# Unused bytes between the buffers of a weight ring, in a fused attention and two-MLP kernel

## The chip, the cores and the metric

One core of a Trainium2 chip runs the whole kernel in one launch. The metric is the device time of that core in microseconds (us). The engines are TensorE (PE; its weight loads are shown as a row of their own, PEld), VectorE (DVE), ScalarE (ACT), GpSimd (POOL) and SyncE (SP), which issues every DMA here.

## The reference, cut to what matters

```python
def _attn_ref(q, k, v):                    # 2 x 12 heads, 448 tokens, head size 64
    scores = where(causal, q @ k.T / 8, -1e9)
    return softmax(scores) @ v

x = attn_out.reshape(896, 768)

def _moe_ref(x, w_in, w_out):              # 768 -> 2048 -> 768
    h = x @ w_in
    return (h * sigmoid(h)) @ w_out

def _moe2_ref(x, w_in, w_out, g_ln):       # 768 -> 1024 -> 768
    h = x @ w_in
    solu = h * softmax(h)
    return (layernorm(solu) * g_ln) @ w_out
```

All in float32. The weights arrive from the host as 64-bit words, and are float64 in value.

## The kernel before, in words

The kernel runs in five stages: the attention, then four matrix products called GEMM1 to GEMM4 here. To keep the precision of float32, each operand of a GEMM is split into a high and a low part in the matmul type fp32r, and each product is three matmuls: high by high, high by low, low by high.

GEMM1 (`gemm1`, lines 304 to 312) multiplies the weights w1 with the attention's result. The weights are the **stationary** operand (loaded into the array, 128 by 128), and the activations `xh` and `xl` are the **moving** operand (448 columns, one batch half). GEMM2 (`mm2`, lines 486 to 492) does the same with w2 and the activations `gh` and `gl`. Each of the two has 96 weight blocks of 128x128, and each block meets two batch halves with three matmuls, so there are 2 x 96 x 2 x 3 = 1,152 matmuls of 448 columns in all, 576 in each GEMM. In GEMM3 (line 606) and GEMM4 (line 661) the sides are changed: the activations are stationary and the weights move, from tiles of their own that stay in place.

The weights of GEMM1 and GEMM2 pass through a **ring**. Each is cut into 32 chunks of 384 columns (three blocks). A chunk is loaded by DMA (`load_w`), put together from its 64-bit words on ACT (line 216) and DVE (lines 221, 227, 237), and split by `split_w` (line 239): ACT writes the high part `wh` (line 247), POOL writes the low part `wl` (line 248). Both come from the pool `wring`, which has 4 buffers for each name, 1,536 bytes per partition each, so that successive chunks take successive buffers and a buffer comes free when the last matmul on the chunk before it in that buffer has read it. All four buffers of a name lie a multiple of 256 bytes apart, since 1,536 is 6 x 256.

The order of the work is written out by hand (`feed`, `feed_to` and the loops from line 437 on). Chunks go round the ring in order; each chunk is used for one batch half (9 matmuls), then for the other (9 matmuls). The first four chunks of GEMM1 and the last four of GEMM2 are visited once for each half at different times.

The kernel already places unused bytes at six spots (`pad`, line 60): they shift the tiles behind them. As the program is built, the activations `xh`, `xl`, `gh` and `gl` start at 224 modulo 256 bytes in a partition and all ring buffers at 160, so the distance from the moving operand to the stationary one is 192 modulo 256 in every matmul of GEMM1 and GEMM2 (steps from block to block and from half to half are multiples of 256). In GEMM3 the moving weights start at 32 and the stationary activations at 224, which is again a distance of 192, with 512 columns. In GEMM4 both start at 0, a distance of 0, with 256, 384 or 512 columns. The transposes of line 641 have a distance of 128.

Of the kernel before, what the change touches and what calls it, by code (L numbers as in the profile page):

```python
# [8 lines left out]
F32 = mybir.dt.float32  # L9
F32R = mybir.dt.float32r  # L10
# [17 lines left out]
CH = 384  # L28
# [15 lines left out]
def fused(ctx, tc, qT, kT, vv, vt, w1, w2, w3, w4, gl, out):  # L44
# [3 lines left out]
    def pool(name, bufs=1, **kw):  # L48
        return tc.alloc_tile_pool(name=name, bufs=bufs, **kw)
# [3 lines left out]
    raw = pool("raw", RAWS)  # L53
    xs = pool("xs", XS)
    gap = pool("gap")
    wring = pool("wring", 4)

    ident = const.tile([128, 128], F32, name="ident")

    def pad(where, count):  # L60
        where.tile([128, count // 4], F32, name="pad", tag="pad", bufs=1)

    pad(act, 64)
    pad(gap, 192)
    xh = act.tile([128, KD, T], F32R, name="xh", tag="ah")
# [3 lines left out]
    with tc.manual_schedule():  # L69
# [169 lines left out]
        def split_w(n, c, dst=None, lo_engine=None):  # L239
            x = wx.pop((n, c))  # L240
            if dst is None:
                h = wring.tile([128, CH], F32R, name="wh", tag="wh")
                l = wring.tile([128, CH], F32R, name="wl", tag="wl")
                wsp[n, c] = (h, l)
            else:
                h, l = dst
            nc.scalar.activation(h, x, AF.Copy)  # L247
            (lo_engine or nc.gpsimd).tensor_tensor(l, x, h.bitcast(F32), ALU.subtract)  # L248
# [22 lines left out]
        def finish(m):  # L271
            n, c = order[m]
            if n < 3:
                split_w(n, c)
            elif n == 4:
                split4(c)
            ready.add(order[m])
# [78 lines left out]
        for i in range(NP2 + TL + 2):  # L356
            live = i < NP2
            n, r, p, x = i - 1, i - TL, i - TL - 1, i - TL - 2
# [180 lines left out]
        for m in range(N3):  # L539
            if m == 10:  # L540
                for a in tail:
                    block2(a, 1)
                evict2(yps[KD - 1, 1], KD - 1, 1)
            sl = slice(CH * m, CH * m + CH)
            split_w(3, m, (w3h[:, sl], w3l[:, sl]), nc.vector if m % 3 else nc.gpsimd)
# [194 lines left out]
```

## Time and profile before

| | |
|---|---|
| median of 3 runs | 442.62 us (442.28 to 442.82) |
| the profiled execution's own time | 442.5 us |
| its span, first to last instruction | 440.7 us |
| what lies around the span | 1.8 us |
| PE, PEld, DVE, ACT, POOL busy | 98%, 87%, 73%, 51%, 39% of the span |

A matmul's duration in the profile (363 ns for 448 columns) runs from its start to the drain of its last column, and the next one starts long before that. The spacing of the starts, read from the timeline, is what a matmul costs here. The stages follow each other: attention until about 90 us, with GEMM1 from there to 200 us, GEMM2 to 315 us, GEMM3 to 374 us and GEMM4 to the end.

### The profile page before, as it was taken

How to read it: one execution, taken by the hardware profiler on the slowest of the kernel's cores; microseconds unless marked ns; L12 is line 12 of the kernel's file. 1: busy time of each engine (PE TensorE's matmuls, PEld its weight loads, DVE VectorE, ACT ScalarE, POOL GpSimd, SP SyncE). 2: the span in 40 equal slices, each digit the busy share in tenths (PEclk: the TensorE clock that was granted, in tenths of full speed). 3: DMA queues.
4: the chain of work that ended last, by engine and by line, in shares of the span. 5: the costliest groups of instructions: out<-in, count | busy, mean ns of one | idle time of the engine just before them, and what ended most of it. 6: DMA issues, size and time to landing. Idle time of an engine off the chain costs nothing.

```text
span 440.7 us, 6969 instructions
## 1 busy us (share of the span) xinstructions
PE 432.4 (98%) x2379; PEld 382.2 (87%) x2379; DVE 321.9 (73%) x705; ACT 223.5 (51%) x519; POOL 170.3 (39%) x197
## 2 busy tenths in 40 slices
PE   8899999999999999999999999999999999999997
PEld 5576777789999999999999999999888888999996
DVE  4988987679999999898785979756978787511110
ACT  4999998344443534344344444433647765712121
POOL 3757655137767777674432424332501000000000
PEclk9999999999999999999999999999999999999999
DMA  5787311205433434333745647564023210010101
GB/s 163 206 251 208 107 37 30 80 0 147 141 110 106 141 83 135 106 111 107 230 136 174 196 150 231 167 188 132 12 72 108 83 61 1 36 37 36 56 36 55
DMA packets 26387, 49.22 MB, mean 112 GB/s; under 512 B 6128, under 2 KB 13936, under 8 KB 26352
## 3 DMA queue, kind: packets, MB, share of 16 engines
q1 hardware_dynamic: 26352, 48.77, 36.8%
q8 instruction: 19, 0.31, 0.3%
q14 instruction: 16, 0.13, 0.1%
HBM read 46.01 MB, written 2.75 MB: 111 GB/s over the span
## 4 chain that ended last, share of the span: by engine, by line
PE 91%; ACT 4%; DVE 4%; issue 0%; DVEq 0%; ACTq 0%
PE h L312 8%; PE h L311 8%; PE h L310 8%; PE h L492 7%; PE h L491 7%; PE h L490 7%; PE ps L663 4%; PE ps L661 4%; PE ps L662 4%; PE h L608 4%; PE h L607 4%; PE h L606 4%; PE pv L193 4%; PE tr L165 3%; ACT e L142 3%; PE sa L125 2%
## 5 line engine op out<-in xcount | busy, mean ns | idle before, releaser
L248 POOL TENSOR_TENSOR wl<-wx,wh 128x384 fp32r<-128x384 f32 x64 | 77.6, 1212 | 95.4 <-ACT wh L247 91.8
L216 ACT ACTIVATE wr<-wr 128x384 f32<-128x384 f32 x96 | 52.5, 554 | 34.5 <-DMA wr<-w_in 34.2
L247 ACT ACTIVATE wh<-wx 128x384 fp32r<-128x384 f32 x64 | 33.5, 523 | 69.8 <-DVE wx L227 40.4
L227 DVE SCALAR_TENSOR_TENSOR wx<-wr,wx 128x384 uint32<-128x384 uint32 x96 | 66.6, 694 | 0.0
L312 PE MATMUL h<-xh,wl 128*128 128x448 f32 x174 | 63.2, 363 | 0.0
L311 PE MATMUL h<-xl,wh 128*128 128x448 f32 x174 | 63.1, 362 | 0.0
L310 PE MATMUL h<-xh,wh 128*128 128x448 f32 x174 | 62.6, 360 | 0.0
L237 DVE TENSOR_SCALAR wr<-wr 128x384 uint32<-128x384 uint32 x96 | 59.6, 621 | 4.1 <-DMA wr<-w_in 4.0
L221 DVE SCALAR_TENSOR_TENSOR wx<-wr 128x384 uint32<-128x384 uint32 x96 | 58.3, 608 | 1.3 <-POOL gl L320 1.3
L492 PE MATMUL h<-gh,wl 128*128 128x448 f32 x160 | 58.1, 363 | 0.0
L491 PE MATMUL h<-gl,wh 128*128 128x448 f32 x160 | 58.0, 362 | 0.0
L490 PE MATMUL h<-gh,wh 128*128 128x448 f32 x160 | 57.6, 360 | 0.0
L320 POOL TENSOR_TENSOR gl<-sg,gh 128x448 fp32r<-128x448 f32 x32 | 40.9, 1279 | 20.7 <-DVE gh L319 10.5
L142 ACT ACTIVATE e<-e,st 128x384 f32<-128x384 f32 (+3 forms) x84 | 43.7, 525 | 8.2 <-DVE st L136 8.2
L152 POOL TENSOR_TENSOR e<-e,st 128x384 f32<-128x384 f32 (+3 forms) x63 | 37.5, 629 | 26.7 <-PE tr L165 16.6
L661 PE MATMUL ps<-w4h,lh 128*128 128x384 f32 (+2 forms) x112 | 38.0, 339 | 0.0
L663 PE MATMUL ps<-w4h,ll 128*128 128x384 f32 (+2 forms) x112 | 37.5, 335 | 0.0
L662 PE MATMUL ps<-w4l,lh 128*128 128x384 f32 (+2 forms) x112 | 37.5, 335 | 0.0
L650 DVE TENSOR_TENSOR ll<-tp,lh 128x512 fp32r<-128x512 f32 x14 | 9.0, 686 | 37.3 <-ACT lh L649 37.3
L311 PEld LDWEIGHTS h<-xl,wh 128*128 128x128 f32 x174 | 32.7, 188 | 2.4
L310 PEld LDWEIGHTS h<-xh,wh 128*128 128x128 f32 x174 | 32.5, 187 | 2.3
L312 PEld LDWEIGHTS h<-xh,wl 128*128 128x128 f32 x174 | 32.7, 188 | 1.8
(100 smaller groups left out, 844.4 us busy)
## 6 DMA issues: line engine op xcount, KB each, us to landing
wr<-w_in SPq DMA_DIRECT2D x96, 384.0 KB, 3.6
k<-kT_in SPq DMA_DIRECT2D x12, 224.0 KB, 3.0
q<-qT_in SPq DMA_DIRECT2D x12, 192.0 KB, 3.1
v<-vv_in SPq DMA_DIRECT2D x12, 192.0 KB, 2.9
out<-o SPq DMA_DIRECT2D x12, 192.0 KB, 1.8
qt<-qT_in SPq DMA_DIRECT2D x24, 16.0 KB, 2.6
v<-vt_in SPq DMA_DIRECT2D x12, 32.0 KB, 2.5
out<-o SPq DMA_DIRECT2D x1, 256.0 KB, 2.0
```

Source lines behind the costliest of these rows:

```text
L142: nc.scalar.activation(ep(p, u), ep(p, u), AF.Exp, bias=st[p][:, 0, n:n + 1], scale=-1.0, accum_out=st[p][:, 1, n:n + 1])
L221: nc.vector.scalar_tensor_tensor(x.bitcast(U32), r[:, :, 1], 0x80000000, r[:, :, 0], ALU.bitwise_and, ALU.bitwise_or)
L227: nc.vector.scalar_tensor_tensor(xu, r[:, :, 1], 3, xu, ALU.logical_shift_left, ALU.bitwise_or)
L237: nc.vector.tensor_scalar(low, low, 29, None, ALU.logical_shift_right)
L248: (lo_engine or nc.gpsimd).tensor_tensor(l, x, h.bitcast(F32), ALU.subtract)
L310: nc.tensor.matmul(ps[:, :S], wh, rh, start=k == 0, stop=False)
L311: nc.tensor.matmul(ps[:, :S], wh, rl, start=False, stop=False)
L312: nc.tensor.matmul(ps[:, :S], wl, rh, start=False, stop=k == KD - 1)
L490: nc.tensor.matmul(ps[:, :S], wh, rh, start=f == 0, stop=False)
L491: nc.tensor.matmul(ps[:, :S], wh, rl, start=False, stop=False)
L492: nc.tensor.matmul(ps[:, :S], wl, rh, start=False, stop=f == KF - 1)
L661: nc.tensor.matmul(ps[:, :w], lh[:, k], w4h[:, k, ns], start=k == 0, stop=False)
```

## The change

The pool `wring` no longer rotates four buffers under one name. Eight tiles are allocated once, four for `wh` and four for `wl`, and `split_w` takes them in turn. Behind each tile lie unused bytes: 32, 96, 96 and 32 for the four of a part, in sum 256.

```diff
-    wring = pool("wring", 4)
+    wring = pool("wring")
...
+    ring = {"wh": [], "wl": []}
+    for part in ring:
+        for space in (32, 96, 96, 32):
+            ring[part].append(wring.tile([128, CH], F32R, name=f"{part}{len(ring[part])}", tag=f"{part}{len(ring[part])}"))
+            wring.tile([128, space // 4], F32, name="pad", tag=f"{part}p{len(ring[part])}")
+    turn = [0]
     pad(act, 64)
     pad(gap, 192)
...
             if dst is None:
-                h = wring.tile([128, CH], F32R, name="wh", tag="wh")
-                l = wring.tile([128, CH], F32R, name="wl", tag="wl")
+                h, l = ring["wh"][turn[0] % 4], ring["wl"][turn[0] % 4]
+                turn[0] += 1
                 wsp[n, c] = (h, l)
```

As built, the four tiles of a part start at 160, 192, 32 and 128 modulo 256, so the distance from the moving operand (224) is 192, 224, 64 and 160 for successive chunks; it is the same for the high and the low part of a chunk. Each distance belongs to 16 of the 64 chunks, which is 288 of the 1,152 matmuls. The ring as a whole grows by 512 bytes, so what lies behind it keeps its place modulo 256. On each of the five engines the instructions and their order are those of before, and so are the number, the semaphores' engines and the values of the waits.

## Rows read from the trace of the kernel before

**Rows 1.** The page: busy time and share of the span of each engine.
```profile
PE 432.4 (98%) x2379; PEld 382.2 (87%) x2379; DVE 321.9 (73%) x705; ACT 223.5 (51%) x519; POOL 170.3 (39%) x197
```

**Rows 2.** The whole answer on who PE waited for (total us, times, longest).
```profile
PE tr L165 <- ACT aT L183: 1.8, 3, 1.2
PE pv L326 <- DVE xl L322: 1.4, 1, 1.4
PE sb L125 <- DVE st L136: 0.7, 2, 0.5
PE pv L193 <- ACT aT L183: 0.7, 1, 0.7
PE sa L125 <- DVE st L136: 0.3, 1, 0.3
```

**Rows 3.** Windows: stretch, busy us (instructions) by engine, clock, DMA share, GB/s.
```profile
core 0: us, PE busy (x) PEld busy (x) DVE busy (x) ACT busy (x) POOL busy (x), PEclk, DMA share, GB/s
100.00:200.00 100.00, 100.00 (x502) 93.73 (x501) 95.28 (x146) 40.90 (x85) 70.13 (x58) 1.00 0.39 118
200.00:310.00 110.00, 110.00 (x552) 103.11 (x551) 83.21 (x156) 47.00 (x94) 39.49 (x32) 1.00 0.57 173
```

**Rows 4.** Timeline of PE in GEMM1: start, us, what; first and last of a stretch.
```profile
99.16 0.36 PE L310 MATMUL h<-xh,wh 128*128 128x448 f32 x1
...
196.36 0.36 PE L310 MATMUL h<-xh,wh 128*128 128x448 f32 x1
```

**Rows 5.** Line 310 between 99.16 and 196.35 us: matmuls, ns min/median/max, first and last start.
```profile
L310 PE MATMUL h<-xh,wh x162: 360/360/360, 99.2 to 195.8; 128*128 128x448 f32 x162
```

**Rows 6.** Timeline of PE in GEMM3: first and last of a stretch.
```profile
339.92 0.39 PE L606 MATMUL h<-w3h,yh 128*128 128x512 f32 x1
...
360.52 0.39 PE L606 MATMUL h<-w3h,yh 128*128 128x512 f32 x1
```

**Rows 7.** Line 606 between 339.92 and 360.51 us.
```profile
L606 PE MATMUL h<-w3h,yh x30: 388/388/388, 339.9 to 359.8; 128*128 128x512 f32 x30
```

**Rows 8.** Timeline of PE in GEMM4, its 512-column slice, and what follows.
```profile
429.04 0.39 PE L661 MATMUL ps<-w4h,lh 128*128 128x512 f32 x1
429.27 0.40 PE L662 MATMUL ps<-w4l,lh 128*128 128x512 f32 x1
429.50 0.40 PE L663 MATMUL ps<-w4h,ll 128*128 128x512 f32 x1
429.74 0.39 PE L661 MATMUL ps<-w4h,lh 128*128 128x512 f32 x1
429.96 0.39 PE L662 MATMUL ps<-w4l,lh 128*128 128x512 f32 x1
430.20 0.40 PE L663 MATMUL ps<-w4h,ll 128*128 128x512 f32 x1
430.43 0.39 PE L661 MATMUL ps<-w4h,lh 128*128 128x512 f32 x1
430.66 0.40 PE L662 MATMUL ps<-w4l,lh 128*128 128x512 f32 x1
430.89 0.39 PE L663 MATMUL ps<-w4h,ll 128*128 128x512 f32 x1
431.12 0.39 PE L661 MATMUL ps<-w4h,lh 128*128 128x512 f32 x1
...
434.52 0.28 PE L661 MATMUL ps<-w4h,lh 128*128 128x256 f32 x1
```

**Rows 9.** The chain that ended last: start, us, what; transposes of 128 columns.
```profile
364.80 0.87 PE tp L641 x8
```

**Rows 10.** The ring's writers: who waited for whom (total us, times, longest).
```profile
POOL wl L248 <- ACT wh L247: 91.8, 42, 6.2
ACT wh L247 <- DVE wx L227: 40.4, 20, 3.7
ACT wh L247 <- PE h L311: 21.8, 14, 2.6
```

## The prediction, made before the changed kernel ran

> **What bounds the kernel now.** I read the busy shares first: PE is busy 98% of the span, the next engine, DVE, 73% [rows 1]. A high busy share of PE can hide gaps, so the second view is who PE waited for. That answer has five rows, all of them on attention lines, 4.9 us in sum, and none on a ring buffer [rows 2]. In GEMM1 and GEMM2 PE is busy in every microsecond of the two windows, at a granted clock of 1.00, which is the 2.4 GHz level [rows 3]. The writers of the ring are the ones that wait: POOL for ACT, ACT for DVE, and ACT for matmuls to set a buffer free [rows 10]. So the two GEMMs that the change touches last exactly as long as the spacing of their matmul starts, and nothing but that spacing can move the time, unless the feeding engines become late.
>
> The third view is the spacing itself. In GEMM1, line 310 starts 162 times between 99.16 and 196.36 us [rows 4, 5]; with lines 311 and 312 that is 486 matmuls in 97.20 us, or **200.0 ns for 448 columns**. At one column a cycle, 448 columns at 2.4 GHz last 186.7 ns, so each matmul pays 13.3 ns on top. GEMM2 does the same: 552 matmuls touch its window of 110.00 us, two of them at its edges [rows 3], which is 200 ns again. In GEMM3, also at distance 192, 90 matmuls of 512 columns take 20.60 us [rows 6, 7], 228.9 ns each; 512 columns last 213.3 ns, so the surplus is 15.6 ns. In GEMM4's last slice, at distance 0, the 24 matmuls start with nine in 2.08 us (231.1 ns each, surplus 17.8) and settle to 15 in 3.40 us (226.7 ns each, surplus 13.3) [rows 8].
>
> **The change part by part.** *Instructions, waits and queues:* none is added, removed or moved on any engine, DMA issues included, and the waits are the same in number and value. Eight fixed tiles in turn come free at the same matmuls as four rotating buffers did. I cost this at nothing. *The writers:* ACT and POOL write the same 384 columns to tiles that start 32, 128 and 224 bytes further modulo 256. Should a write get slower, the cover is their own waiting, 91.8 us of POOL and 40.4 plus 21.8 us of ACT [rows 10]; if the cover were gone, PE would wait for `wl` or `wh` in rows that are absent today.
>
> *The addresses:* the moving stream and the load of the next weights read the same partitions at the same time. A quarter of the matmuls, 288, keeps distance 192 and its 200.0 ns. The other 864 get distances 224, 64 and 160, which the trace has nowhere for fp32r. The bounds come from the nearest rows.
>
> - Below: the surplus of 13.3 ns need not be a floor. The plain fp32 transposes, at distance 128, take 0.87 us for eight [rows 9], 108.8 ns each; at two cycles a column 128 columns last 106.7 ns, which leaves a surplus of 2.1. So a distance could give back up to 13.3 - 2.1 = 11.2 ns.
> - Above: a distance at which the surplus doubles would cost 13.3 ns.
> - Between: GEMM3 settles 228.9 - 226.7 = 2.2 ns above GEMM4 at the same width, and the unsettled start of GEMM4's slice runs 231.1 - 226.7 = 4.4 ns above it.
>
> That 13.3 ns appears exactly, at distance 192 with 448 columns and at distance 0 with 512, makes it look like what remains when the two streams have settled without meeting; GEMM3 then shows a distance and width that settle less well. I take GEMM3's 2.2 ns for each of the three new distances, because it is the only settled spacing above that level: 864 x 2.2 = **1.9 us**.
>
> *The borders:* PE now changes distance at each change of chunk. 64 chunks, eight of them visited twice, make 72 visits and 71 borders. If streams have to settle anew, the row nearest is the start of GEMM4's slice: 2.08 us where nine settled matmuls take 2.04, so 0.04 us at most, and nothing at least. Half of that at 71 borders is **1.4 us**.
>
> The sum is 1.9 + 1.4 = 3.3 us on the profiled execution's 442.5 us: **445.8 us**. The median of the runs, 442.62 us, is 0.1 above that execution, which changes nothing here. A measurement of this kernel can tell about 0.2%, 0.9 us, from no change.
>
> What hides is little: PE is the bound, so added spacing goes to the end in full, and the feeders gain slack. Late next, if PE got faster, is DVE, 95.28 us busy in 100 us of GEMM1 [rows 3].
>
> **The rivals.**
>
> *No effect.* The surplus is the same 13.3 ns at distances 0 and 192 and at widths of 448 and 512, which speaks for a fixed cost without regard to address; GEMM3's extra 2.2 ns would then come from something else in that stage. The time would be 442.5 us. Against it stands that plain fp32 pays only 2.1 ns, so the surplus depends on how fast the moving operand is read, as a meeting of two streams would. The unsettled start of GEMM4's slice, in the same stage with the same code, speaks against it too. The case in which the spaces do not lead to different distances gives the same time; the addresses of the built program leave it no chance. The Trainium skill, "TensorE: Matmul & The Clock Gate", section "Part 2: What happens when you issue a matmul", says that TensorE reads the moving operand and the weights through two independent ports, so that loading the next weights takes no read bandwidth from the running matmul. By that rule this rival would be certain, with 442.5 us; the trace disagrees in part, since a matmul with a load beside it is 13.3 ns over its columns in fp32r.
>
> *Faster.* The 13.3 ns are the meeting of the two streams, and 192 and 0 are both bad distances. One good distance among the three gives back 288 x 11.2 = 3.2 us (439.3 us); all three 9.7 us (432.8 us), near where DVE's 95% would stop GEMM1. It decides for faster from a mean of 0.8 ns gained over the 1,152 matmuls. For it: fp32's 2.1 ns. Against it: two different distances give the same surplus, and every other mean spacing of fp32r matmuls read above lies over it.
>
> *One very bad distance.* A distance at which the loads always meet the stream doubles the surplus: 288 x 13.3 = 3.8 us, with 576 x 2.2 = 1.3 for the others and 1.4 for the borders 6.5 us, so 449.0 us. Nothing in the trace shows such a spacing settled; the single intervals in GEMM4's start reach 0.24 us against 0.227.
>
> **How the numbers follow.** Slower by over 0.2%: 0.60, of which 0.47 for the forecast with its bounds (0.9 us up to 864 x 4.4 + 71 x 0.04 = 6.6 us, so 443.4 to 449.1) and 0.13 for very bad distances (449.0, and 452.2 were it two: 576 x 13.3 + 288 x 2.2 + 1.4 = 9.7 us). No effect within 0.2%: 0.26. Faster: 0.14. The range leaves out the faster rival and the far end of very bad distances, under 0.2 together: 441.9 to 450.0 us. The likeliest case's own range is 443.4 to 449.1.
>
> **What would show it right or wrong.** Right: in GEMM1's timeline the 18 starts of a chunk, 3.60 us today, fall into four classes that repeat with every fourth chunk; one stays near 3.60, others are longer by about 0.04 us (18 x 2.2 ns), with the first matmuls of a chunk above the rest. GEMM3, GEMM4 and the attention keep their lengths. DVE, ACT and POOL keep the length of one instruction, and PE still waits for no ring buffer. Wrong on the size: a class 0.24 us longer (18 x 13.3 ns). Wrong on the mechanism: all chunks at 3.60 us (no effect), a class below 3.60 us (faster), or a wait of PE for `wh` or `wl`, which would make the writers the cause.

## The result, and the profile after

The changed kernel takes **446.58 us** (446.48 to 446.71, four runs) against 442.63 us before: a ratio of 1.0087, 95% interval 1.0073 to 1.0101. It is slower by 3.95 us; the span of its profiled execution grew from 440.7 to 444.7 us.

Busy time on the page of the changed kernel, to be set against [rows 1]:

```profile
PE 436.4 (98%) x2379; PEld 382.5 (86%) x2379; DVE 321.5 (72%) x705; ACT 223.6 (50%) x519; POOL 170.0 (38%) x197
```

The instructions are as many as before. PE's busy time grew by 4.0 us, as much as the span, and no other compute engine's by more than 0.1. So neither a wait nor a slower writer is the cause, and the next two views say the same. The first is who PE waited for, which has the same five lines and the same sums as [rows 2]; the first of the five:

```profile
PE tr L171 <- ACT aT L189: 1.8, 3, 1.2
```

The second is the writer of the ring's high part (ns min/median/max); before, its median on ACT was 526 ns too, and the median of POOL's low part is 1,137 ns in both traces:

```profile
L253 ACT ACTIVATE wh<-wx x64: 504/526/528, 37.2 to 304.9; 128x384 fp32r<-128x384 f32 x64
```

The time is in the spacing. The windows that answer to [rows 3] still have PE busy throughout, with 494 and 543 matmuls in them instead of 502 and 552:

```profile
100.00:200.00 100.00, 100.00 (x494) 92.30 (x493) 93.14 (x143) 41.27 (x86) 69.06 (x58) 1.00 0.40 118
200.00:310.00 110.00, 110.00 (x543) 101.50 (x542) 84.19 (x156) 45.10 (x89) 39.66 (x32) 1.00 0.56 166
```

PE's timeline in GEMM1 shows where. Each of these rows is the first matmul of a chunk (18 matmuls); the distances in turn are 192, 224, 64, 160, twice over, and the last row begins the next round:

```profile
128.81 0.36 PE L316 MATMUL h<-xh,wh 128*128 128x448 f32 x1
...
132.41 0.37 PE L316 MATMUL h<-xh,wh 128*128 128x448 f32 x1
...
136.09 0.36 PE L316 MATMUL h<-xh,wh 128*128 128x448 f32 x1
...
139.73 0.37 PE L316 MATMUL h<-xh,wh 128*128 128x448 f32 x1
...
143.43 0.36 PE L316 MATMUL h<-xh,wh 128*128 128x448 f32 x1
...
147.03 0.37 PE L316 MATMUL h<-xh,wh 128*128 128x448 f32 x1
...
150.74 0.37 PE L316 MATMUL h<-xh,wh 128*128 128x448 f32 x1
...
154.38 0.37 PE L316 MATMUL h<-xh,wh 128*128 128x448 f32 x1
...
158.08 0.36 PE L316 MATMUL h<-xh,wh 128*128 128x448 f32 x1
```

| distance | us a chunk, first round | second round | over 3.60 |
|---|---|---|---|
| 192 | 3.60 | 3.60 | 0 |
| 224 | 3.68 | 3.71 | 0.08 and 0.11 |
| 64 | 3.64 | 3.64 | 0.04 |
| 160 | 3.70 | 3.70 | 0.10 |

This pair of rounds repeats through both GEMMs, except at the two ends, where a chunk is visited for one batch half at a time. Sixteen rounds, half with 0.22 us and half with 0.25, come to 3.76 us by these readings. Counted from the first start of GEMM1 to the last of GEMM2, the trace itself grew by 3.6 us (from 241.1 us, 73.88 to 314.96, to 244.7 us, 74.10 to 318.83), of the span's 4.0.

### The profile page after: what moved, and what is told of

Its sections match the earlier page's. It is cut to its first block, busy times and chain, and to the rows that moved or that the text cites. A ratio compares the mean times of both kernels' runs of the same rounds, so it can differ in the third digit from the quotient of the medians.

```text
span 444.7 us, 6969 instructions
## 1 busy us (share of the span) xinstructions
PE 436.4 (98%) x2379; PEld 382.5 (86%) x2379; DVE 321.5 (72%) x705; ACT 223.6 (50%) x519; POOL 170.0 (38%) x197
## 4 chain that ended last, share of the span: by engine, by line
PE 91%; ACT 4%; DVE 4%; issue 0%; DVEq 0%; ACTq 0%
PE h L316 8%; PE h L317 8%; PE h L318 8%; PE h L496 7%; PE h L497 7%; PE h L498 7%; PE ps L669 4%; PE ps L667 4%; PE ps L668 4%; PE h L613 4%; PE h L614 4%; PE h L612 4%; PE pv L199 4%; PE tr L171 3%; ACT e L148 3%; PE sa L131 2%
## 5 line engine op out<-in xcount | busy, mean ns | idle before, releaser
L316 PE MATMUL h<-xh,wh 128*128 128x448 f32 x174 | 63.6, 365 | 0.0
L496 PE MATMUL h<-gh,wh 128*128 128x448 f32 x160 | 58.5, 366 | 0.0
```

The costliest lines, as they stand in the source:

```text
L316: nc.tensor.matmul(ps[:, :S], wh, rh, start=k == 0, stop=False)
L496: nc.tensor.matmul(ps[:, :S], wh, rh, start=f == 0, stop=False)
```

## The experiments

The question was what a chunk's spacing follows from. Theory A: from its own distance. Theory B: from the change of distance between chunks. Theory C: fixed tiles cost something in place of rotating buffers. More came up as results arrived, among them D, a distance has one or several settled spacings and the way PE enters picks one, and F, the address of the tile itself and not its distance from the moving operand.

### One distance for all chunks: 192, 224, 64, 160

The tiles lie without spaces, shifted together; `s` is 0, 32, 128 and 224.

```diff
-        for space in (32, 96, 96, 32):
...
+    wring.tile([128, s // 4], F32, name="pad", tag="front")      # none where s is 0
+    for part in ring:
+        for n in range(4):
+            ring[part].append(wring.tile([128, CH], F32R, name=f"{part}{n}", tag=f"{part}{n}"))
+    wring.tile([128, (512 - s) // 4], F32, name="pad", tag="back")
```

> Eight fixed ring tiles as in the change, but no spaces between them, so that all 1,152 matmuls keep distance 192; the spaces' 512 bytes lie behind the ring in one piece. Theory A (each distance has a settled spacing of its own): 200.0 ns everywhere and the time of before, 442.6 us within 0.3. Theory B (the change of distance between chunks costs): the same. Theory C (the fixed tiles in place of rotating buffers cost something): slower, up to the change's 446.6 us.

Measured: 442.84 us, ratio 1.0001 (0.9991 to 1.0010). Theory C falls: fixed tiles cost nothing, and the whole loss is the addresses'.

> All ring tiles shifted by 128 bytes, distance 64 everywhere. In the changed kernel's trace a chunk at this distance took 3.64 us. Theory A: 1,152 x 2.2 ns = 2.6 us, so 445.2 us. Theory B: 442.6 us.

Measured: 445.23 us, ratio 1.0060 (1.0043 to 1.0077).

> All ring tiles shifted by 224 bytes, distance 160 everywhere. In the changed kernel's trace a chunk at this distance took 3.69 to 3.70 us. Theory A: 1,152 x 5.2 ns = 6.0 us, so 448.6 us. Theory B: 442.6 us.

Measured: 448.74 us, ratio 1.0137 (1.0122 to 1.0153). For these two theory A held to 0.2 us, and B fell. PE's timeline for one chunk at distance 64, then for one at 160: 3.64 and 3.70 us, as in the change, though no chunk here has a neighbour at another distance.

```profile
106.22 0.37 PE L317 MATMUL h<-xh,wh 128*128 128x448 f32 x1
...
109.86 0.37 PE L317 MATMUL h<-xh,wh 128*128 128x448 f32 x1
```

```profile
106.98 0.37 PE L317 MATMUL h<-xh,wh 128*128 128x448 f32 x1
...
110.68 0.36 PE L317 MATMUL h<-xh,wh 128*128 128x448 f32 x1
```

> All ring tiles shifted by 32 bytes, so that every matmul of GEMM1 and GEMM2 has distance 224. In the changed kernel's trace a chunk of 18 at this distance took 3.68 or 3.72 us in turn, against 3.60 at 192. Theory A: that spacing holds throughout, 1,152 x 4.6 to 6.4 ns = 5.3 to 7.4 us, so 448.0 to 450.0 us. Theory B: no change of distance, so no loss, 442.6 us.

Measured: 442.80 us, ratio 1.0003 (0.9994 to 1.0013). Here A missed by more than 5 us: distance 224 alone cost nothing in this kernel. Three pieces of its timeline tell why. The columns are start, us, what; the first piece is seven spacings of the first GEMM1 matmuls, which run between attention steps, the second eight spacings of the next such piece, the third one chunk later on:

```profile
74.34 0.37 PE L318 MATMUL ps<-xl,wh 128*128 128x448 f32 x1
...
75.77 0.36 PE L319 MATMUL ps<-xh,wl 128*128 128x448 f32 x1
...
82.99 0.37 PE L317 MATMUL ps<-xh,wh 128*128 128x448 f32 x1
...
84.65 0.37 PE L319 MATMUL ps<-xh,wl 128*128 128x448 f32 x1
...
99.42 0.36 PE L317 MATMUL h<-xh,wh 128*128 128x448 f32 x1
...
103.02 0.36 PE L317 MATMUL h<-xh,wh 128*128 128x448 f32 x1
```

1.43 us over 7 is 204 ns, 1.66 over 8 is 207.5 (to the timeline's 0.01 us), 3.60 over 18 is 200.0. One kernel at one distance shows three spacings, two of them those of the change's 3.68 and 3.71 us chunks (204.4 and 206.1 ns). After a break in the stream PE came in another way, and it then kept 200.0 ns to the end of GEMM2. That is theory D: at one distance and with no neighbour at another, the way PE entered goes with the spacing.

### Two distances in turn, and the change's tiles in another order

```diff
-        for space in (32, 96, 96, 32):
+        for space in (0, 32, 0, 224):                    # two distances; no pad where 0
...
-                h, l = ring["wh"][turn[0] % 4], ring["wl"][turn[0] % 4]
+                at = (0, 2, 1, 3)[turn[0] % 4]           # other order: (0, 2, 3, 1), old spaces
+                h, l = ring["wh"][at], ring["wl"][at]
```

> A ring of fixed tiles with two distances in turn, 192 and 224, instead of four. Alone, 224 ran at 200.0 ns throughout; within the change, entered from 192, its chunks took 3.68 and 3.72 us in turn. Theory D (at 224 there are several settled spacings, and the phase in which the streams enter a chunk picks one): the 32 chunks at 224 enter from 192 as in the change and take 3.68 or 3.72 us, 32 x 0.08 to 0.12 = 2.6 to 3.8 us, so 445.3 to 446.5 us, with the 192 chunks at 3.60. Theory E (the loss at 224 belongs to the four-distance cycle, such as what 64 or 160 leave behind two chunks earlier): 442.7 us.

Measured: 446.29 us, ratio 1.0087 (1.0072 to 1.0102). A chunk at 224, then one at 192, on PE's timeline:

```profile
132.46 0.36 PE L318 MATMUL h<-xh,wh 128*128 128x448 f32 x1
...
136.17 0.37 PE L318 MATMUL h<-xh,wh 128*128 128x448 f32 x1
...
139.78 0.36 PE L318 MATMUL h<-xh,wh 128*128 128x448 f32 x1
```

That is 3.71 and 3.61 us. Theory E falls: no 64 or 160 is needed. Either distance alone was free in its kernel above, and the two in turn lose as much as the change does. Behind a break between attention steps, though, a chunk at 224 took 200 ns a matmul in this kernel too, 1.40 us for seven spacings of the second chunk:

```profile
81.46 0.36 PE L319 MATMUL ps<-xl,wh 128*128 128x448 f32 x1
...
82.86 0.37 PE L320 MATMUL ps<-xh,wl 128*128 128x448 f32 x1
```

Behind a chunk at 192 in a stream without breaks, chunks at 224 took 206 (3.71 us above). So one kernel has two spacings at one distance.

> The tiles of the change at the same addresses, taken in another order: distances 192, 64, 160, 224. Theory D: chunks at 64 stay at 3.64 us and at 160 at 3.69 to 3.70, which is 16 x 0.04 + 16 x 0.095 = 2.2 us; the chunks at 224 now enter from 160 and can take 3.60, 3.68 or 3.72, so the time is 444.9 us with all at 3.60 and 446.5 with the change's mean. Theory A' (a distance of 224 costs 0.10 us a chunk whenever other distances stand beside it): 446.5 us, with 3.68 and 3.72 in turn.

Measured: 446.68 us, ratio 1.0096 (1.0081 to 1.0111). One round, distances 192, 64, 160, 224:

```profile
129.00 0.37 PE L317 MATMUL h<-xh,wh 128*128 128x448 f32 x1
...
132.61 0.37 PE L317 MATMUL h<-xh,wh 128*128 128x448 f32 x1
...
136.25 0.37 PE L317 MATMUL h<-xh,wh 128*128 128x448 f32 x1
...
139.95 0.37 PE L317 MATMUL h<-xh,wh 128*128 128x448 f32 x1
...
143.66 0.37 PE L317 MATMUL h<-xh,wh 128*128 128x448 f32 x1
```

3.61, 3.64, 3.70, 3.71 us: the first three keep their price in the new order. The total does not tell D from A', since 224 entered from 160 goes to its slowest spacing. It goes there in every whole round, though, where A' had 3.68 and 3.72 in turn.

### The moving operand shifted, not the ring

```diff
-    pad(act, 64)
-    pad(gap, 192)
+    pad(act, 96)
+    pad(gap, 160)
```

> The ring as in u192 at its old addresses; the moving operand of GEMM1 is shifted by 32 bytes instead, so that GEMM1 has distance 160, GEMM2 keeps 192, and GEMM3, whose stationary operand lies in the same place, has 224. Theory D (the distance decides): GEMM1 at 205.3 ns as in u160, 576 x 5.3 = 3.0 us, GEMM2 at 200.0; GEMM3 between 226.7 and what it has, 228.9, or up to 6 ns above. In all 445.2 to 447.3 us. Theory F (the address of the ring's tile itself decides): GEMM1 stays at 200.0 ns, about 442.7 us.

Measured: 446.12 us, ratio 1.0085 (1.0068 to 1.0102). A chunk of GEMM1 (3.70 us at distance 160) and 18 matmuls of GEMM3 (4.20 at 224, where [rows 6, 7] give 4.12 for as many at 192):

```profile
102.61 0.37 PE L316 MATMUL h<-xh,wh 128*128 128x448 f32 x1
...
106.31 0.37 PE L316 MATMUL h<-xh,wh 128*128 128x448 f32 x1
...
330.22 0.40 PE L612 MATMUL h<-w3h,yh 128*128 128x512 f32 x1
...
334.42 0.40 PE L612 MATMUL h<-w3h,yh 128*128 128x512 f32 x1
```

Theory F falls: the ring lies where it lay, and GEMM1 pays the price of 160. GEMM3 at 224 costs 4.4 ns a matmul more than at 192, 252 x 4.4 = 1.1 us.

### The distances not yet seen

Three kernels built like the first four, with `s` of 64 (`u0`), 96 (`tab1`) and 192 (`tab2`). In the last two the operand of GEMM1 moves as well:

```diff
-    pad(act, 64)
-    pad(gap, 192)
+    pad(gap, 256)          # tab1
...
+    pad(act, 128)          # tab2
+    pad(gap, 128)
```

> Distance 0 everywhere in GEMM1 and GEMM2. Theory D with GEMM4's rows (distance 0, 173.3 ns at 384 and 226.7 at 512 columns, 13.3 over the columns): 200.0 ns and 442.7 us. If the width decides as much as the distance: another settled spacing, 0 to 7 ns longer, up to 450.7 us.

Measured: 445.15 us, ratio 1.0064 (1.0049 to 1.0079). GEMM4's surplus did not carry over; the time is 2.45 us above the 442.7. A chunk at distance 0 took 3.65 us:

```profile
106.23 0.36 PE L317 MATMUL h<-xh,wh 128*128 128x448 f32 x1
...
109.88 0.36 PE L317 MATMUL h<-xh,wh 128*128 128x448 f32 x1
```

> Three untried distances in one kernel: the ring shifted by 96 bytes and the operand of GEMM1 by 64 back, so GEMM1 has distance 96, GEMM2 32 and GEMM3 128 (its stationary operand lies where GEMM1's moving one did). If 200.0 ns at 448 columns and 226.7 at 512 are floors: each stage at or over them, 442.6 - 0.6 (GEMM3 down to its floor) = 442.0 us at best, and up to 205.3 ns in both GEMMs, about 449 us. If some distance gives back part of the 13.3 ns: a stage under 200.0 ns.

Measured: 445.52 us, ratio 1.0065 (1.0050 to 1.0080). GEMM1 at 96, then GEMM2 at 32:

```profile
106.63 0.36 PE L316 MATMUL h<-xh,wh 128*128 128x448 f32 x1
...
110.23 0.36 PE L316 MATMUL h<-xh,wh 128*128 128x448 f32 x1
...
240.49 0.36 PE L496 MATMUL h<-gh,wh 128*128 128x448 f32 x1
...
244.15 0.36 PE L496 MATMUL h<-gh,wh 128*128 128x448 f32 x1
```

No stage came under its floor, and GEMM3, at distance 128, ran at about 232 ns for 512 columns (4.17 us for 18 matmuls, from 334.09 to 338.26), above the 228.9 of before.

> The ring at distance 128 from GEMM2's operand; GEMM1's operand shifted by 64 bytes on, so GEMM1 has distance 64 and GEMM3 0. GEMM1: 202.2 ns as in u64, 1.3 us. GEMM2: 200.0 to 205.3 ns, 0 to 3.1 us. GEMM3: 226.7 ns if distance 0 settles there as in GEMM4's last slice, 252 x 2.2 = 0.55 us less than before; if the stationary and moving sides' arrays differ, up to 233 ns, 1.1 us more. In all 443.3 to 448.1 us.

Measured: 445.97 us, ratio 1.0077 (1.0062 to 1.0092). GEMM2 at 128, then 18 matmuls of GEMM3 at 0:

```profile
241.89 0.36 PE L497 MATMUL h<-gh,wh 128*128 128x448 f32 x1
...
245.56 0.36 PE L497 MATMUL h<-gh,wh 128*128 128x448 f32 x1
...
339.62 0.39 PE L613 MATMUL h<-w3h,yh 128*128 128x512 f32 x1
...
343.70 0.39 PE L613 MATMUL h<-w3h,yh 128*128 128x512 f32 x1
```

All eight distances, in us for 18 matmuls of 448 columns:

| 0 | 32 | 64 | 96 | 128 | 160 | 192 | 224 |
|---|---|---|---|---|---|---|---|
| 3.65 | 3.66 | 3.64 | 3.60 | 3.67 | 3.70 | 3.60 | 3.60, 3.68 or 3.72 |

None settles below 3.60, 200.0 ns a matmul. No step finer than 32 bytes was tried. The value at 0 is not that of GEMM4 [rows 8], whose surplus at distance 0 and 512 columns is 13.3 ns where 448 columns have 202.8 - 186.7 = 16.1. So the distance alone does not set the surplus: the width has a say, or the exchange of sides that goes with it in GEMM3 and GEMM4, where the weights move. The runs do not separate the two.

### A single chunk at another distance

```diff
+            ring[part].append(wring.tile([128, CH + 8 * (n == 0)], F32R, name=f"{part}{n}", tag=f"{part}{n}"))
+        wring.tile([128, 224 // 4], F32, name="pad", tag=f"{part}p")
...
+                if turn[0] % 4 == 0:
+                    cut = slice(0, CH) if turn[0] == 12 else slice(8, CH + 8)
+                    h, l = h[:, cut], l[:, cut]
```

> As u224, distance 224 throughout, which ran at 200.0 ns, but one chunk of the 64, the thirteenth of GEMM1, is written 32 bytes earlier in its tile and so has distance 192. Theory D (several settled spacings at 224; the phase of entry picks one, and PE stays in it until something disturbs it): 3.60 us a chunk until there, 3.60 for the chunk at 192, and from the next one on 3.68 to 3.72 us for the 51 chunks that are left, although all of them are at 224: 51 x 0.08 to 0.12 = 4.2 to 6.0 us, so 447.0 to 448.7 us. Theory G (a chunk's spacing follows from its own distance and its neighbours', and recovers): 442.8 to 443.0 us.

Measured: 448.87 us, ratio 1.0141 (1.0124 to 1.0158). The total is D's, but the course is not the one that I expected. The rows are seven spacings between attention steps, a chunk ahead of the odd one, the odd chunk (129.46 to 133.07) and the one behind it:

```profile
74.45 0.36 PE L320 MATMUL ps<-xl,wh 128*128 128x448 f32 x1
...
75.85 0.37 PE L321 MATMUL ps<-xh,wl 128*128 128x448 f32 x1
...
99.70 0.37 PE L319 MATMUL h<-xh,wh 128*128 128x448 f32 x1
...
103.42 0.37 PE L319 MATMUL h<-xh,wh 128*128 128x448 f32 x1
...
129.46 0.37 PE L319 MATMUL h<-xh,wh 128*128 128x448 f32 x1
...
133.07 0.36 PE L319 MATMUL h<-xh,wh 128*128 128x448 f32 x1
...
136.78 0.37 PE L319 MATMUL h<-xh,wh 128*128 128x448 f32 x1
```

PE ran at 200 ns in the early piece (1.40 us over 7), where the kernel with 224 alone ran at 204, and had fallen into 3.72 us a chunk by 99.70, where the other one took 3.60, long before the odd chunk. That one took 3.61 us, and behind it the 3.71 to 3.72 came back. So the test did not show one chunk causing the loss. It showed theory G wrong: chunks at 224 among chunks at 224 take 3.60 us in one kernel and 3.72 in the other, a difference of 6 us in the time, and this kernel by itself has both 200 and 206.7 ns there. One thing besides the odd chunk differs between the two: the low parts of the ring lie 256 bytes further from the high ones here, as they do in the change, in the two-distance kernel and in the one with the other order. Of the five kernels with chunks at 224, only the one without this shift kept 200.0 ns. The shift is not the whole cause: without it the early pieces took 204 and 207 ns, and with it the early pieces here and in the two-distance kernel took 200. Whether it helped to pick the spacing was not tried.

### GEMM3 at distance 0

```diff
-        pad(w3p, 192)
+        pad(w3p, 256)
```

> The kernel before, with the bytes behind GEMM3's weights 256 instead of 192, so that GEMM3 has distance 0 and all else stays. In tab2's trace GEMM3 took 4.08 us for 18 matmuls at distance 0, against 4.12 at 192 in the kernel before: 14 x 0.04 = 0.56 us less, so 442.0 us where before is at 442.6, a ratio of 0.9987. If GEMM3 is held by its feeders or the gain is lost in the waits at its tiles' ends: no change.

Measured: 442.48 us, ratio 0.9995 (0.9986 to 1.0004), which can't be told from no change. The matmuls did speed up, and a longer wait took part of it. PE's timeline, with its load row and the instruction of ACT that released it:

```profile
323.59 0.39 PE L606 MATMUL h<-w3h,yh 128*128 128x512 f32 x1
...
327.67 0.39 PE L606 MATMUL h<-w3h,yh 128*128 128x512 f32 x1
...
331.71 0.19 ACT L628 ACTIVATION_READ_ACCUMULATOR h<-e,s 128x1 f32 x1
...
331.95 0.19 PEld L606 LDWEIGHTS h<-w3h,yh 128*128 128x128 f32 x1 [0.46 <-ACT h L628]
331.95 0.50 PE L606 MATMUL h<-w3h,yh 128*128 128x512 f32 x1
```

The first two rows are 18 matmuls in 4.08 us, the expected 0.04 less than before. The load that starts at 331.95 has waited 0.46 us, where the kernel before has one such wait of 0.2 us, for a result buffer `h` that ACT used last, until 331.71 + 0.19. From its first start to the first of GEMM4, GEMM3 became shorter by 0.21 us (59.39 to 59.17), not by 0.56. A stage that runs faster reaches the next bound in it.

## Why the prediction was right

The time, 446.58 us, lies 0.8 us above the 445.8 forecast and inside the range. The place was as forecast, and so was the mechanism that carries the loss, a spacing that differs with the address. That the sum came so near is partly luck: one term was half of what it measured, and the other measured nothing of its kind. Taken step by step:

- *What bounds the kernel:* right. PE's busy time took the whole of the loss, with no wait for the ring, and instructions, writers and fixed tiles cost nothing (the run at 192 throughout, 1.0001).
- *The addresses, 864 x 2.2 ns = 1.9 us:* the right term, mis-sized. The three distances cost 4.4 to 6.1, 2.2 and 5.6 ns a matmul by the rows, 3.76 us in sum. GEMM3's row fitted distance 64 alone. The unsettled spacing of GEMM4's start, 4.4 ns, which I kept as a bound, was nearer to the mean.
- *The borders, 71 x 0.02 us = 1.4 us:* wrong as a term. Chunks at 64 and 160 cost the same with and without other neighbours, so there is no settling price at a border that adds up. The two errors nearly cancelled, by luck. Entering a chunk matters in another way, which the step did not have: at 224 it picks the spacing for the whole chunk, 0.08 or 0.11 us instead of nothing, and this is 8 x 0.19 = 1.5 of the 3.76 us. So one of the four classes repeats with every eighth chunk, not with every fourth as forecast.
- *No effect:* refuted. Its main support, the same 13.3 ns at 0 and 192, came from comparing two widths: at 448 columns distance 0 has 16.1. The rule of the Trainium skill, "TensorE: Matmul & The Clock Gate", section "Part 2: What happens when you issue a matmul", that a load on its own port takes no read bandwidth from the running matmul, promised 442.5 us; the runs disagree with that time, since addresses alone moved it by up to 1.4% (448.87 us).
- *Faster:* no distance settled under 200.0 ns, so nothing of the surplus came back. That 200.0 ns is a floor is what eight distances in steps of 32 bytes show, for 448 columns and this order of matmuls.
- *One very bad distance:* no distance cost more than 6.7 ns at 448 columns (3.72 us a chunk), half of the 13.3 assumed.

What picks a spacing at 224 stays open, and so does the cause beneath: that the two reads meet in the memory is argued from the prices following the distance whichever side is moved (3.70 us a chunk at 160 both ways), and no run looks at the reads themselves.

## What to carry to other kernels

Where PE is busy without a gap, read the spacing of matmul starts from the timeline against the columns at the granted clock, and try the relative placement of the two operands modulo 256 bytes; here it was worth 0 to 1.4%. Give all buffers of a ring the same distance, and choose one that keeps its spacing after every entry, as 192 did, rather than one that only ran well once, as 224 did. Price such an edit with a run of each distance by itself and with one of the mixture, because they can differ.

## What was not expected of the hardware

Matmuls of one shape, at one distance and the same granted clock, had one of three spacings: 200.0, about 204.5 and 206.7 ns at distance 224. The first and the last were kept for more than 180 us without a break, each in a kernel of its own; the middle one was seen for a single chunk at a time. Two kernels whose chunks stood at that distance, all in one and all but one in the other, took 442.80 and 448.87 us, each in all of its runs (442.15 to 443.15 and 448.24 to 450.25).
